# A decode layer on one core: q rows of four groups in four TensorE column groups, h summed in SBUF, a fourth transpose bank, another TensorE order, contiguous FFN stationaries

## The chip, the cores and the metric

The kernel runs on one core of one Trainium2 chip. The metric is the device time of one execution in microseconds (us).

In the views PE is TensorE, PEld its weight loads, ACT is ScalarE and DVE is VectorE, the two engines that here copy TensorE's results out of its PSUM banks into SBUF, the core's memory; SPq is the queue that issues loads and stores. L433 is line 433 of the kernel, x28 a count of instructions. The lines of TensorE (before / after) are: L433 transposes of K, L516 / L518 scores, L538 and L546 / L540 and L573 softmax columns and sums, L561 / L560 products with V, L575 o_columns, L637 / L645 the two FFN input products, L660 / L668 the product with w_down.

## The reference

One decode step of a transformer layer, batch 2, model width 640: layer norm, attention of 32 heads (head width 192) over the last 2,048 cached keys and values, output projection with residual, layer norm, GEGLU feed-forward (FFN) of width 1,536 with residual. Inputs and outputs are bf16.

```
h  = x + attention(layernorm(x), K[:, :, -2048:], V[:, :, -2048:], wq) @ wo
h2 = h + (gelu(layernorm(h) @ w_gate) * (layernorm(h) @ w_up)) @ w_down
```

K and V of the window are 64 tiles each (one per head and batch), 786 KB a tile. With the weights the kernel reads 122.3 MB.

## The kernel before

All loads are issued by one queue (SP) in a fixed order into a ring in SBUF of 110,592 bytes per partition, 18 tiles of K or V. A load may be issued when everything that lies in its place has been used. The order is K of the next group, V of this group, wo of this group, with a block of wq before every fourth K group, and the FFN weights last. A group is four tiles: two heads, two batches (the prediction says "four heads").

```python
GRAN = 768
RING = 18 * 6144
...
        def pump():
            while queue:
                key, off, nbytes, src, shape, i = queue[0]
                old = [q for q in live if q[1] < off + nbytes and off < q[1] + q[2]]
                if any(q[0] not in used for q in old):
                    return
                ...
                toks = [("ring", x) for x in range(off // GRAN, (off + nbytes + GRAN - 1) // GRAN)]
                P.op("sp", lambda e, v=v, src=src: e.dma_start(v, src), W=toks + [("sem", i % NSEM)], ...)
...
            wd = B_w_down.rearrange("(p f) n -> p f n", f=NF)
            for i in range(3):
                load(("wd", i), 2 * 4 * D, wd[:, 4 * i:4 * i + 4, :], ...)
```

The tokens are the kernel's own bookkeeping of who wrote which piece of the ring, in pieces (granules) of 768 bytes. A load waits for the last writer of each of its granules. K, V, wo and wq have sizes that are multiples of 768. The three parts of w_down, 5,120 bytes each, are not, so neighbouring parts share a granule.

TensorE does nearly everything else. K tiles are transposed as f32 pairs into three PSUM banks, which ACT and DVE evict:

```python
        def q_rows(g):                       # [2 x 384]: q of one group, both batches
            for c in range(NC5):
                e.matmul(m1[0:2, 128:512], lhsT=xnT[:, c, :], rhs=wq[:, c, off:off + 384], ...)
            # then ACT copies m1 to qrow
...
        for n in range(4):
            transposes(n)
        for g in range(4):
            q_rows(g)
        q_stationary(0); scores(0); softmax(0); e_columns(0)
        for g in range(NG):                  # 16 groups
            if g + 1 < NG:
                for j in range(4):
                    transposes(4 * (g + 1) + j)
                    if (g + 1) % 4 == 0:
                        q_rows(g + 1 + j)
                q_stationary(g + 1)
            pv(g, 0)
            if g + 1 < NG: scores(g + 1)
            pv(g, 1); pv(g, 2)
            if g + 1 < NG: softmax(g + 1)
            pv(g, 3)                         # and ACT copies the sums to osb
            o_columns(g)
            if g + 1 < NG: e_columns(g + 1)
            oproj(g)                         # accumulates in PSUM bank hps over all groups
        ...
        def ffn_in(bank, key):
            for f in range(NF):
                for c in range(NC5):
                    e.matmul(bank[:, 2 * f:2 * f + 2], lhsT=wv[:, c, f:F:NF], rhs=hnT[:, c, :], ...)
```

## Time and profile before

| | before |
|---|---|
| device time, median of 3 runs | 324.76 us |
| span of the profiled run (its time: 325.54 us) | 323.8 us |
| TensorE busy, mean granted clock | 79%, 0.869 |
| bytes read, mean rate over the span | 122.3 MB, 378 GB/s |

The first view is the page's picture of the kernel before in 40 equal slices (8.1 us each): busy tenths of TensorE, granted TensorE clock in tenths, busy tenths of the DMA engines, and what they moved.

```profile
PE   3665778788887978797887979797987879797784
PEclk9997797979799786979799897979796898979555
DMA  7999999999999999999999999999999999998310
GB/s 274 416 416 414 419 417 416 410 409 419 413 391 329 422 413 419 411 412 414 414 386 413 418 414 417 407 418 414 413 368 419 419 414 415 414 427 371 104 66 0
```

The DMA row says that the engines are busy nearly all the time, and the GB/s row shows small dips. The second view, the waits of TensorE (released by, then us in total, number, longest):

```profile
PE m L575 <- ACT osb L570: 16.1, 16, 1.1
PE tps L433 <- ACT ktr L448: 8.9, 36, 0.3
PE m L546 <- DVE ering L545: 8.4, 16, 0.5
PE m L525 <- DVE mrhs L316: 7.0, 16, 1.1
```

No line of the full waits table before has TensorE waiting for a load. It waits for ACT and DVE, about 16 us, 9 us, 8 us and 7 us. Third, one group in the timeline of TensorE (start, duration, instructions; in brackets the idle time ahead of it and who ended it):

```profile
206.64 0.39 PE L525 MATMUL m<-mrhs,pm 128*128 128x4 f32 x2 [0.41 <-DVE mrhs L316]
206.96 0.52 PE L561 MATMUL ops<-ring,ering 128*32 128x192 bf16 x16
208.53 1.21 PE L575 MATMUL m<-sel,osb 128*128 128x2 f32 x6 [1.06 <-ACT osb L570]
...
210.50 0.38 PE L546 MATMUL m<-zrhs,hm 128*128 128x2 f32 x2 [0.53 <-DVE ering L545]
...
211.34 4.92 PE L433 MATMUL tps<-identf,ring 128*128 128x128 f32 x28
...
217.39 1.53 PE L433 MATMUL tps<-identf,ring 128*128 128x128 f32 x12 [0.26 <-ACT ktr L448]
```

The waits come one after another, and then the transposes run slowly: 28 in 4.92 us at first, then 12 in 1.53 us. The clock record has half the clock (0.50) from 211.85 to 215.27 us. One such group takes 17.03 us. Last, the end of the kernel in the timeline:

```profile
300.40 2.60 PE L561 MATMUL ops<-ring,ering 128*32 128x192 bf16 x64
300.95 5.00 SPq L265 DMA_DIRECT2D ring<-in_B_w_down_dram  x2
309.14 3.72 PE L637 MATMUL sps<-hnT,ring 128*128 128x2 bf16 x60 [0.80 <-DVE hnT L320]
312.71 3.69 PE L637 MATMUL ops<-hnT,ring 128*128 128x2 bf16 x60
316.69 2.56 PE L660 MATMUL m<-uT,ring 128*128 128x2 bf16 x60 [0.28 <-DVE uT L320]
319.49 0.41 SPq L668 DMA_DIRECT2D out_dram<-yT  x1
```

The last products with V (L561) end at 303 us. The completion records of the loads in the trace put the landing of the last V tile at 289.0 us: TensorE is 14 us behind. The parts of w_down land at 300.9, 305.6 and 309.5 us, each issued when the one before has landed.

### The profile page before, as it was taken

What the parts mean: (1) busy time and instruction counts of PE and PEld (TensorE: products, weight loads), DVE (VectorE), ACT (ScalarE), POOL (GpSimd) and SP (SyncE); (2) the same over time, 40 slices, a digit from 0 to 9 for tenths busy, and PEclk for the clock granted to TensorE, in tenths of its full rate; (3) what the DMA queues carried; (4) which work ended last, traced back from release to release, by engine and by line L of the source; (5) the groups of instructions that cost most, each with busy time, mean ns of one, the idle gap of its engine ahead of it and who ended that gap; (6) DMA issues with size and microseconds to landing.
All of it is one profiled execution on the core that took longest, in us unless ns stands there. A gap on an engine that the chain in (4) does not pass through costs nothing.

```text
span 323.8 us, 6976 instructions
## 1 busy us (share of the span) xinstructions
PE 255.5 (79%) x3105; PEld 203.3 (63%) x3105; DVE 126.1 (39%) x340; ACT 112.8 (35%) x150; POOL 3.2 (1%) x9
## 2 busy tenths in 40 slices
PE   3665778788887978797887979797987879797784
PEld 3642758585565858585755758585656757585683
DVE  5621544435343534344342535343333525353120
ACT  2341433324281423333271524243351615242000
POOL 4000000000000000000000000000000000000000
PEclk9997797979799786979799897979796898979555
DMA  7999999999999999999999999999999999998310
GB/s 274 416 416 414 419 417 416 410 409 419 413 391 329 422 413 419 411 412 414 414 386 413 418 414 417 407 418 414 413 368 419 419 414 415 414 427 371 104 66 0
DMA packets 24385, 122.74 MB, mean 379 GB/s; under 512 B 2722, under 2 KB 2724, under 8 KB 24100
## 3 DMA queue, kind: packets, MB, share of 16 engines
q1 hardware_dynamic: 24356, 122.31, 93.3%
q8 instruction: 24, 0.39, 0.5%
q14 instruction: 5, 0.04, 0.0%
HBM read 122.29 MB, written 0.00 MB: 378 GB/s over the span
## 4 chain that ended last, share of the span: by engine, by line
PE 59%; ACT 24%; DVE 12%; issue 3%; POOL 0%; ACTq 0%; POOLq 0%
PE tps L433 27%; ACT ktr L448 16%; PE sps L516 8%; PE m L575 6%; PE m L461 4%; ACT eexp L529 4%; DVE mx L521 3%; PE hps L589 3%; DVE ering L545 2%; PE m L546 2%; PE m L525 2%; ACT osb L570 2%; ACT qrow L466 2%; PE m L538 1%; DVE mrhs L316 1%
## 5 line engine op out<-in xcount | busy, mean ns | idle before, releaser
L433 PE MATMUL tps<-identf,ring 128*128 128x128 f32 x768 | 124.3, 326 | 11.8 <-ACT ktr L448 8.9
L433 PEld LDWEIGHTS tps<-identf,ring 128*128 128x128 f32 x768 | 109.2, 170 | 24.9 <-ACT ktr L448 17.8
L448 ACT ACTIVATE ktr<-tps 128x1024 bf16<-128x1024 bf16 x80 | 80.1, 1022 | 116.2 <-PE tps L433 114.9
L452 DVE COPY ktr<-tps 128x1024 bf16<-128x1024 bf16 x112 | 75.5, 689 | 69.6 <-PE tps L433 68.9
L575 PE MATMUL m<-sel,osb 128*128 128x2 f32 x96 | 19.9, 324 | 16.1 <-ACT osb L570 16.1
L529 ACT ACTIVATE eexp<-sps,nm 128x512 bf16<-128x512 f32 x16 | 11.0, 687 | 59.3 <-DVE nm L527 59.3
L575 PEld LDWEIGHTS m<-sel,osb 128*128 128x128 f32 x96 | 18.6, 270 | 19.9 <-ACT osb L570 19.9
L561 PE MATMUL ops<-ring,ering 128*32 128x192 bf16 x1024 | 30.7, 253 | 0.0
L516 PE MATMUL sps<-ktr,rq 128*32 128x512 bf16 x384 | 26.0, 405 | 5.4 <-ACT ktr L448 4.6
L561 PEld LDWEIGHTS ops<-ring,ering 128*32 128x32 bf16 x1024 | 21.8, 98 | 3.8
L521 DVE TENSOR_REDUCE mx<-sps 128x1 f32<-128x512 f32 x16 | 11.1, 691 | 31.0 <-PE sps L516 31.0
L516 PEld LDWEIGHTS sps<-ktr,rq 128*32 128x32 bf16 x384 | 9.7, 97 | 16.5 <-DVE rq L320 8.6
L461 PE MATMUL m<-ring,xnT 128*2 128x384 bf16 x80 | 17.7, 357 | 2.7 <-ACT qrow L466 2.7
L320 DVE TENSOR_TENSOR rq<-m,mask 128x24 bf16<-128x24 f32 x64 | 7.2, 175 | 18.5 <-PE m L486 18.5
L466 ACT ACTIVATE qrow<-m 2x768 bf16<-2x768 f32 x16 | 12.6, 790 | 4.9 <-PE m L461 4.9
L546 PE MATMUL m<-zrhs,hm 128*128 128x2 f32 x32 | 6.5, 274 | 8.4 <-DVE ering L545 8.4
L320 DVE TENSOR_TENSOR ot<-m,rinv 128x6 bf16<-128x6 f32 x16 | 2.6, 164 | 26.6 <-PE m L575 26.6
L461 PEld LDWEIGHTS m<-ring,xnT 128*2 128x2 bf16 x80 | 5.7, 87 | 11.4 <-ACT qrow L466 4.4
L589 PEld LDWEIGHTS hps<-ot,ring 128*128 128x128 bf16 x240 | 12.1, 134 | 0.3 <-DVE ot L320 0.3
L546 PEld LDWEIGHTS m<-zrhs,hm 128*128 128x128 f32 x32 | 5.2, 203 | 11.4 <-DVE ering L545 11.4
L525 PEld LDWEIGHTS m<-mrhs,pm 128*128 128x128 f32 x32 | 4.8, 188 | 11.3 <-DVE mrhs L316 11.3
L589 PE MATMUL hps<-ot,ring 128*128 128x2 bf16 x240 | 11.6, 177 | 0.3 <-DVE ot L320 0.3
(79 smaller groups left out, 104.6 us busy)
## 6 DMA issues: line engine op xcount, KB each, us to landing
ring<-in_A_k_cache_dram SPq DMA_DIRECT2D x64, 768.0 KB, 14.4
ring<-in_A_v_cache_dram SPq DMA_DIRECT2D x64, 768.0 KB, 15.9
ring<-in_A_wq_dram SPq DMA_DIRECT2D x4, 1920.0 KB, 14.4
ring<-in_A_wo_dram SPq DMA_DIRECT2D x16, 480.0 KB, 14.0
ring<-in_B_w_gate_dram SPq DMA_DIRECT2D x1, 1920.0 KB, 15.3
ring<-in_B_w_up_dram SPq DMA_DIRECT2D x1, 1920.0 KB, 13.4
ring<-in_B_w_down_dram SPq DMA_DIRECT2D x3, 640.0 KB, 4.6
xrow<-in_A_x_dram SPq DMA_DIRECT2D x1, 2.5 KB
```

Source lines behind the costliest of these rows:

```text
L433: ins = e.transpose(tps[bi][:, 128 * u:128 * (u + 1)], kv[:, off:off + 128], identf[:, :])
L448: act(lambda e, c=c, kslot=kslot, bv=bv: e.activation(out=ktr[:, kslot, c, :], in_=bv[:, 0:1024], func=ACT.Copy), W=[("kt", kslot, c)], X= ...
L452: dve(lambda e, c=c, kslot=kslot, bv=bv: e.tensor_copy(ktr[:, kslot, c, :], bv[:, 0:1024]), W=[("kt", kslot, c)], X=[("t", bi)])
L461: ins = e.matmul(m1[0:2, 128:512], lhsT=xnT[:, c, :], rhs=wq[:, c, off:off + 384], start=(c == 0), stop=(c == NC5 - 1))
L466: act(lambda e: e.activation(out=qrow[0:2, g % QS, :, 0:rep, :], in_=m1[0:2, 128:512].rearrange("p (h d) -> p h d", h=2).unsqueeze(2).to_b ...
L516: ins = e.matmul(sps[32 * j:32 * (j + 1), :], lhsT=rq[:, g % 2, j, k, :], rhs=r, start=(k == 0), stop=(k == 5), tile_position=(0, 32 * j))
L521: dve(lambda e: e.tensor_reduce(out=mx[:, :], in_=sps[:, :], axis=AX.X, op=ALU.max), W=["mx"], X=["s"])
L529: act(lambda e: e.activation(out=eexp[:, :], in_=sps[:, :], func=ACT.Exp, bias=nm[:, 0:1], scale=1.0, accum_out=zr[:, 0:1]), R=["nm"], W=[ ...
L546: pe(lambda e: e.matmul(m2[:, 8:10], lhsT=hm[:, :], rhs=zrhs[:, :], start=True, stop=True), R=["hm", "zrhs"], X=["m2"])
L561: ins = e.matmul(ops_[32 * r:32 * (r + 1), 192 * hh:192 * (hh + 1)], lhsT=ering[:, g % 2, col:col + 32], rhs=vv[:, DH * t:DH * (t + 1)], s ...
L575: ins = e.matmul(m1[:, 32 + 2 * kk:34 + 2 * kk], lhsT=osb[:, kk:384:3], rhs=sel[:, :], start=True, stop=True)
L589: ins = e.matmul(hps[:, 2 * c:2 * c + 2], lhsT=wo[:, kk, c:D:NC5], rhs=ot[:, kk, :], start=(g == 0 and kk == 0 and c == 0), stop=(g == NG ...
```

## The change

The intent is to shorten TensorE's work and to take its waits away:

- q rows of four groups are made at once, each group in its own 32-column strip of the array (xnT is padded to 32 columns), with one ACT copy. A wq block is free after one step.
- The softmax columns, o_columns and oproj of the group before are placed between the transposes of the next group, so that DVE and ACT have time to feed them.
- h is summed in SBUF by a small DVE add per group. That frees the PSUM bank hps for a fourth transpose bank.
- The stationaries of the FFN input products are contiguous (columns 128f to 128f+127 instead of every twelfth). To match, w_down is loaded with rows f·128+p: four runs of 1,280 bytes per partition and part instead of one of 5,120.

```diff
-            wd = B_w_down.rearrange("(p f) n -> p f n", f=NF)
+            wd = B_w_down.rearrange("(f p) n -> p f n", p=128)
...
-                    ins = e.matmul(m1[0:2, 128:512], lhsT=xnT[:, c, :], rhs=wq[:, c, off:off + 384],
-                                   start=(c == 0), stop=(c == NC5 - 1))
+                    for r in range(4):
+                        ins = e.matmul(m1[32 * r:32 * (r + 1), 128:512], lhsT=xnT[:, c, :],
+                                       rhs=wq[:, c, 384 * r:384 * (r + 1)], start=(c == 0), stop=(c == NC5 - 1),
+                                       tile_position=(0, 32 * r))
...
-                        ins = e.matmul(hps[:, 2 * c:2 * c + 2], lhsT=wo[:, kk, c:D:NC5], rhs=ot[:, kk, :],
-                                       start=(g == 0 and kk == 0 and c == 0), stop=(g == NG - 1 and kk == 2),
+                        ins = e.matmul(m1[:, 48 + 2 * c:50 + 2 * c], lhsT=wo[:, kk, c:D:NC5], rhs=ot[:, kk, :],
+                                       start=(kk == 0 and c == 0), stop=(kk == 2), skip_group_check=True)
+            dve(tt(hT..., m1[:, 48:58], old..., ALU.add), ...)        # shortened
...
+            if nxt: transposes(4 * g + 4)                             # shortened from here
+            e_columns(g)
+            if nxt: transposes(4 * g + 5)
+            if g > 0: o_columns(g - 1)
+            if nxt and (g + 1) % 4 == 0: q_rows((g + 1) // 4)
+            if nxt: transposes(4 * g + 6)
+            if g > 0: oproj(g - 1)
+            if nxt: transposes(4 * g + 7); q_stationary(g + 1)
+            pv(g, 0); pv(g, 1)
+            if nxt: scores(g + 1)
+            pv(g, 2); pv(g, 3)
+            if nxt: softmax(g + 1)
...
-                        ins = e.matmul(bank[:, 2 * f:2 * f + 2], lhsT=wv[:, c, f:F:NF], rhs=hnT[:, c, :],
+                        ins = e.matmul(bank[:, 2 * f:2 * f + 2], lhsT=wv[:, c, 128 * f:128 * (f + 1)], rhs=hnT[:, c, :],
```

More of the change, by code (lines that the diff above doesn't have):

```diff
@@ L148 @@
 NSEM = 32
-QS = 5
 def bass_sequential_preLN__sliding_block_cached__geglu_ffn__decode_kernel(
@@ L208, in bass_sequential_preLN__sliding_block_cached__geglu_ffn__decode_kernel @@
         lt = sb("lt", [128, 2, B], F32)
-        xnT = sb("xnT", [128, NC5, B], BF16)
+        xnT = sb("xnT", [128, NC5, 32], BF16)
         hnT = sb("hnT", [128, NC5, B], BF16)
         hT = sb("hT", [128, NC5, B], F32)
-        qrow = sb("qrow", [128, QS, 2, rep, DH], BF16)
+        qrow = sb("qrow", [128, 2, 2, rep, DH], BF16)
         rq = sb("rq", [128, 2, 4, 6, 32], BF16)
@@ L217, in bass_sequential_preLN__sliding_block_cached__geglu_ffn__decode_kernel @@
         zr = sb("zr", [128, 1], F32)
-        zrhs = sb("zrhs", [128, 2], F32)
+        zrhs = sb("zrhs", [128, 2, 2], F32)
         rinv = sb("rinv", [128, 2], F32)
@@ L228, in bass_sequential_preLN__sliding_block_cached__geglu_ffn__decode_kernel @@
         uT = sb("uT", [128, NF, B], BF16)
-        tps = [ps(f"tps{i}", [128, 512], F32) for i in range(3)]
+        tps = [ps(f"tps{i}", [128, 512], F32) for i in range(4)]
         sps = ps("sps", [128, 512], F32)
         ops_ = ps("ops", [128, 512], F32)
-        hps = ps("hps", [128, 512], F32)
         m1 = ps("m1", [128, 512], F32)
@@ L352, in bass_sequential_preLN__sliding_block_cached__geglu_ffn__decode_kernel @@
         act(lambda e: e.preload_act_table_set("natural_log_exp_and_others"))
+        dve(lambda e: e.memset(xnT[:, :, :].rearrange("p a b -> p (a b)").bitcast(I32), 0), W=["xnT"])
         def layernorm(src, src_tok, dst, dst_tok):
@@ L369, in layernorm @@
             act(lambda e: e.activation(out=lt[:, 1, :], in_=lt[:, 0, :], func=ACT.Exp, scale=-0.5), R=["lt0"], W=["lt1"])
-            dve(tt(dst[:, :, :], dT[:, 0, :, :], lt[:, 1, :].unsqueeze(1).to_broadcast([128, NC5, B]), ALU.mult),
+            dve(tt(dst[:, :, 0:B], dT[:, 0, :, :], lt[:, 1, :].unsqueeze(1).to_broadcast([128, NC5, B]), ALU.mult),
                 R=["dT0", "lt1"], W=[dst_tok])
@@ L422, in transposes @@
             for c in range(3):
-                bi = tb_count[0] % 3
+                bi = tb_count[0] % 4
                 tb_count[0] += 1
@@ L453, in transposes, with q_rows @@
                         W=[("kt", kslot, c)], X=[("t", bi)])
-        def q_rows(g):
-            wq, wtoks = where["wq", g // 4]
-            off = 384 * (g % 4)
+        def q_rows(J):
+            wq, wtoks = where["wq", J]
             def fn(e):
                 for c in range(NC5):
-                    ins = e.matmul(m1[0:2, 128:512], lhsT=xnT[:, c, :], rhs=wq[:, c, off:off + 384],
-                                   start=(c == 0), stop=(c == NC5 - 1))
+                    for r in range(4):
+                        ins = e.matmul(m1[32 * r:32 * (r + 1), 128:512], lhsT=xnT[:, c, :],
+                                       rhs=wq[:, c, 384 * r:384 * (r + 1)], start=(c == 0), stop=(c == NC5 - 1),
+                                       tile_position=(0, 32 * r))
                 return ins
             pe(fn, R=["xnT"] + wtoks, X=["m1"])
+            done(("wq", J))
             act(lambda e: e.activation(
-                out=qrow[0:2, g % QS, :, 0:rep, :],
-                in_=m1[0:2, 128:512].rearrange("p (h d) -> p h d", h=2).unsqueeze(2).to_broadcast([2, 2, rep, DH]),
-                func=ACT.Copy, scale=SCALE), W=[("qrow", g % QS)], X=["m1"])
-            if g % 4 == 3:
-                done(("wq", g // 4))
+                out=qrow[:, J % 2, :, 0:rep, :],
+                in_=m1[:, 128:512].rearrange("p (h d) -> p h d", h=2).unsqueeze(2).to_broadcast([128, 2, rep, DH]),
+                func=ACT.Copy, scale=SCALE), W=[("qrow", J % 2)], X=["m1"])
         def q_stationary(g):
-            qx = qrow[0:2, g % QS, :, 0:rep, :].rearrange("p h r d -> p h (r d)")
+            p0 = 32 * (g % 4)
+            qx = qrow[p0:p0 + 2, (g // 4) % 2, :, 0:rep, :].rearrange("p h r d -> p h (r d)")
             nk = 6 if words else 3
@@ L485, in fn @@
                             l = qx[:, h, 128 * k:128 * (k + 1)]
-                        ins = e.matmul(m1[:, col:col + 2], lhsT=l, rhs=identb[0:2, 0:2], start=True, stop=True)
+                        ins = e.matmul(m1[:, col:col + 2], lhsT=l, rhs=identb[p0:p0 + 2, p0:p0 + 2], start=True,
+                                       stop=True, tile_position=(p0, 0))
                 return ins
-            pe(fn, R=[("qrow", g % QS), "identb"], X=["m1"])
+            pe(fn, R=[("qrow", (g // 4) % 2), "identb"], X=["m1"])
             for h in range(2):
@@ L530, in softmax @@
                                        accum_out=zr[:, 0:1]), R=["nm"], W=["eexp", "zr"], X=["s"])
-            dve(ts(zrhs[:, :], oh_b[:, :], zr[:, 0:1], ALU.mult), R=["oh_b", "zr"], W=["zrhs"])
+            dve(ts(zrhs[:, g % 2, :], oh_b[:, :], zr[:, 0:1], ALU.mult), R=["oh_b", "zr"], W=[("zrhs", g % 2)])
         def e_columns(g):
@@ L545, in e_columns @@
             dve(lambda e: e.tensor_copy(dst, src), W=[("er", g % 2)], X=["m2"])
-            pe(lambda e: e.matmul(m2[:, 8:10], lhsT=hm[:, :], rhs=zrhs[:, :], start=True, stop=True),
-               R=["hm", "zrhs"], X=["m2"])
-            dve(lambda e: e.reciprocal(rinv[:, :], m2[:, 8:10]), W=["rinv"], X=["m2"])
         def pv(g, j):
@@ L573, in fn @@
             def fn(e):
+                e.matmul(m1[:, 40:42], lhsT=hm[:, :], rhs=zrhs[:, g % 2, :], start=True, stop=True)
                 for kk in range(3):
@@ L577, in fn @@
                 return ins
-            pe(fn, R=["osb", "sel"], X=["m1"])
+            pe(fn, R=["osb", "sel", "hm", ("zrhs", g % 2)], X=["m1"])
+            dve(lambda e: e.reciprocal(rinv[:, :], m1[:, 40:42]), W=["rinv"], X=["m1"])
             dve(tt(ot[:, :, :], m1[:, 32:38].rearrange("p (k b) -> p k b", b=2),
@@ L588, in fn @@
                     for c in range(NC5):
-                        ins = e.matmul(hps[:, 2 * c:2 * c + 2], lhsT=wo[:, kk, c:D:NC5], rhs=ot[:, kk, :],
-                                       start=(g == 0 and kk == 0 and c == 0), stop=(g == NG - 1 and kk == 2),
-                                       skip_group_check=True)
+                        ins = e.matmul(m1[:, 48 + 2 * c:50 + 2 * c], lhsT=wo[:, kk, c:D:NC5], rhs=ot[:, kk, :],
+                                       start=(kk == 0 and c == 0), stop=(kk == 2), skip_group_check=True)
                 return ins
-            pe(fn, R=wtoks + ["ot"], X=["h"])
+            pe(fn, R=wtoks + ["ot"], X=["m1"])
             done(("wo", g))
+            old, tok = (xT, "xT") if g == 0 else (hT, "hT")
+            dve(tt(hT[:, :, :].rearrange("p c b -> p (c b)"), m1[:, 48:58], old[:, :, :].rearrange("p c b -> p (c b)"),
+                   ALU.add), R=[tok], W=["hT"], X=["m1"])
         for n in range(4):
             transposes(n)
-        for g in range(4):
-            q_rows(g)
+        q_rows(0)
         q_stationary(0)
@@ L604, in bass_sequential_preLN__sliding_block_cached__geglu_ffn__decode_kernel @@
         softmax(0)
-        e_columns(0)
         for g in range(NG):
-            if g + 1 < NG:
-                for j in range(4):
-                    transposes(4 * (g + 1) + j)
-                    if (g + 1) % 4 == 0:
-                        q_rows(g + 1 + j)
+            nxt = g + 1 < NG
+            if nxt:
+                transposes(4 * g + 4)
+            e_columns(g)
+            if nxt:
+                transposes(4 * g + 5)
+            if g > 0:
+                o_columns(g - 1)
+            if nxt and (g + 1) % 4 == 0:
+                q_rows((g + 1) // 4)
+            if nxt:
+                transposes(4 * g + 6)
+            if g > 0:
+                oproj(g - 1)
+            if nxt:
+                transposes(4 * g + 7)
                 q_stationary(g + 1)
             pv(g, 0)
-            if g + 1 < NG:
+            pv(g, 1)
+            if nxt:
                 scores(g + 1)
-            pv(g, 1)
             pv(g, 2)
-            if g + 1 < NG:
+            pv(g, 3)
+            if nxt:
                 softmax(g + 1)
-            pv(g, 3)
-            o_columns(g)
-            if g + 1 < NG:
-                e_columns(g + 1)
-            oproj(g)
-        dve(tt(hT[:, :, :].rearrange("p c b -> p (c b)"), hps[:, 0:10], xT[:, :, :].rearrange("p c b -> p (c b)"),
-               ALU.add), R=["xT"], W=["hT"], X=["h"])
+        o_columns(NG - 1)
+        oproj(NG - 1)
         layernorm(hT, "hT", hnT, "hnT")
```

## The prediction

> **What bounds the kernel now.** Two things at nearly the same pace. (1) The load queue: the stretches table shows the 16 DMA engines at a share of 1.0 and about 416 GB/s from 4 us to 296 us, except dips at 96-104, 168-172 and 240-244 us. Completed loads follow each other at 1.885 us per 786 KB tile of K or V (417 GB/s; the Trainium skill, "DMA: Bandwidth & Descriptors", section "Where 436 GB/s comes from", gives 435 as the ceiling, so little is left), 1.19 per wo, 4.89 per wq, 4.6 per FFN input matrix. (2) TensorE: the waits table shows no TensorE wait for data at all. It takes 17.03 us per group of four heads and 20.5 with q_rows, that is 71.6 us per four groups; the loads need 70.0. TensorE lags: the last V tile has landed by about 289 us, its product ends at 303. The chain of waits is TensorE, evictions and softmax (59% PE, 24% ACT, 12% DVE).
>
> At the end, w_down comes in three loads whose ring slots share a bookkeeping granule, so each is issued only when the one before has landed: 300.9, 305.6, 309.5 us.
>
> **What the change does.**
> - q_rows: four rounds of 0.97 us on TensorE plus 0.9 us of waiting for ACT (19.1 to 26.5 us in the timeline) become one of about 1.2 plus 0.8. About 5 us at the start, 2.5 in each of three later groups. wq is freed earlier, so the dip at 96-104 us should go.
> - PE order: takes away, per group, the 1.0 us wait for osb, 0.5 for the zrhs product, most of 0.4 before scores, and part of the 0.5 us eviction stalls (fourth bank). The half-clock stretch after each (0.57-0.7 at the start of each transpose phase; "TensorE: Matmul & The Clock Gate", Part 1, says idle windows gate the clock, and this trace agrees) should shrink. Estimate: 13-15 us of TensorE work per group, about 25 us less in all.
> - h in SBUF: one more 0.17 us DVE add per group, hidden.
> - Contiguous FFN stationaries: 60 matmuls from 3.7 toward 2.6 us each time, but off the path afterwards. w_down now comes as 512 runs of 1,280 B instead of 128 of 5,120 per load. 3,072 B packets take 125 ns and 6,144 B ones 236, so about 60 ns each: +0.35 us per load, perhaps +0.5.
>
> **On the critical path.** The 25 us are not earned: the kernel becomes bound by its loads. Nominal load times in order put w_down's first landing at 293.9 us; instruction fetches delay the stream by about 3.5 (6.9 us of excess are seen before, of which 3.5 near 100 us are ring stalls that go); the smaller runs add 0.4: about 298. Then two serial loads (4.7 and 3.9 before) at about 5.1 and 4.4: 307.6. The last 20 matmuls 1.1, yT and the output 4.5: span 313.2. Measured times lie about 1 us above the span: **314.0 us**, 80% range 311.0 to 318.5. Chances: faster by over 2% 0.88, within 2% 0.10, slower 0.02.
>
> **What would show it.** TensorE waits for loads of K, V and w_down; the ring waits of the queue (97 us for transposes now) collapse; DMA share 1.0 up to 296 us without the dip near 100; w_gate's product starts near 293 us instead of 309; the FFN input products get shorter without moving the end; the chain of waits ends with the third w_down load.
>
> **What would make it wrong.** Evictions on ACT (1.02 us for five of twelve banks) or a half clock during data waits keep TensorE above 17.5 us per group (then 318-322). Small runs cost more than estimated in the serial w_down loads (316-318). Instruction fetches disturb less (311).

## The result, and the profile after

The changed kernel takes 313.88 us (median of 4 runs, 313.73 to 314.2); before took 324.81 (4 runs, 324.13 to 325.04). The ratio is 0.9668, 95% interval 0.9651 to 0.9685. A ratio is the mean time of one kernel's fast runs over that of the other's fast runs of the same rounds, so it is not quite the ratio of the medians. The span of the profiled run is 312.0 us, the mean clock 0.848.

The page's picture of the changed kernel (slices of 7.8 us):

```profile
PE   3769795826988595955989597945959795976632
PEclk9999899975999787796999778895977889795555
DMA  7999999999999999999999999999999999999732
GB/s 272 415 416 413 417 416 417 414 405 417 417 415 416 413 417 415 418 403 417 417 415 415 417 414 415 418 406 417 414 417 417 414 415 413 417 414 431 320 116 82
```

The dips in GB/s are gone (no slice in the middle under 403), and TensorE now has slices with five tenths of work or less. The waits of TensorE have changed kind:

```profile
PE tps L433 <- DMA ring<-in_A_k_cache_dram: 42.0, 15, 7.1
PE ops L560 <- DMA ring<-in_A_v_cache_dram: 13.1, 13, 1.4
PE m L668 <- DMA ring<-in_B_w_down_dram: 7.2, 2, 4.1
PE m L527 <- DVE mrhs L314: 3.7, 8, 1.1
```

Three kinds of load account for 62 us of TensorE's waiting; there were none before. The last V tile lands at 286.6 us, and its product comes right behind it. The end of the kernel in the timeline:

```profile
286.62 0.83 PE L560 MATMUL ops<-ring,ering 128*32 128x192 bf16 x16 [1.06 <-DMA ring<-in_A_v_cache_dram]
294.29 1.76 PE L645 MATMUL sps<-hnT,ring 128*128 128x2 bf16 x60 [0.80 <-DVE hnT L318]
297.02 1.76 PE L645 MATMUL ops<-hnT,ring 128*128 128x2 bf16 x60 [0.97 <-DMA ring<-in_B_w_up_dram]
298.62 4.62 SPq L263 DMA_DIRECT2D ring<-in_B_w_down_dram  x2
302.92 0.93 PE L668 MATMUL m<-uT,ring 128*128 128x2 bf16 x20 [4.15 <-DMA ring<-in_B_w_down_dram]
306.91 1.76 PE L668 MATMUL m<-uT,ring 128*128 128x2 bf16 x40 [3.05 <-DMA ring<-in_B_w_down_dram]
308.91 0.39 SPq L676 DMA_DIRECT2D out_dram<-yT  x1
```

And the last pieces of the chain of waits, in order of time (start, us, what; 144 pieces, of which the last DMA pieces and the last matmuls are shown):

```profile
273.33 25.27 DMA ring<-in_B_w_down_dram
...
298.62 4.17 DMA ring<-in_B_w_down_dram
...
302.87 3.99 DMA ring<-in_B_w_down_dram
...
306.91 1.77 PE m L668 x40
```

The chain ends in three w_down loads in a row. The first lands in the full stream. The other two are each issued after the one before has landed and take 4.2 and 4.0 us, for 655 KB that the full stream delivers in about 1.6 us. A detail that the prediction had not seen: the product of the first part starts at 302.92, when the *second* part has landed, and the last 40 matmuls start together. The shared granule makes readers wait for the neighbour's load as well.

### The profile page after: what moved, and what is told of

Its sections match the earlier page's. It is cut to its first block, busy times and chain, and to the rows that moved or that the text cites. A ratio compares the mean times of both kernels' runs of the same rounds, so it can differ in the third digit from the quotient of the medians.

```text
span 312.0 us, 7012 instructions
## 1 busy us (share of the span) xinstructions
PE 225.7 (72%) x3105; PEld 195.1 (63%) x3105; DVE 125.8 (40%) x356; ACT 105.9 (34%) x138; POOL 3.2 (1%) x9
## 4 chain that ended last, share of the span: by engine, by line
DMA 72%; PE 20%; SPq 6%; issue 1%; DVE 0%
DMA ring<-in_A_k_cache_dram 50%; PE tps L433 12%; DMA ring<-in_A_v_cache_dram 12%; DMA ring<-in_B_w_down_dram 11%; SPq L263 6%; PE m L575 2%; PE ops L560 1%; PE sps L518 1%; PE m L590 1%; PE m L540 1%; PE m L668 1%; PE m L487 0%; PE m L461 0%; PE m L573 0%; SPq L320 0%
## 5 line engine op out<-in xcount | busy, mean ns | idle before, releaser
L433 PE MATMUL tps<-identf,ring 128*128 128x128 f32 x768 | 121.1, 320 | 44.4 <-DMA ring<-in_A_k_cache_dram 42.0
L569 ACT ACTIVATE osb<-ops 128x384 f32<-128x384 f32 x16 | 7.8, 490 | 57.2 <-PE ops L560 57.2
L580 DVE RECIPROCAL rinv<-m 128x2 f32<-128x2 f32 x16 | 2.7, 170 | 31.2 <-PE m L575 31.2
L590 PEld LDWEIGHTS m<-ot,ring 128*128 128x128 bf16 x240 | 11.8, 129 | 1.1 <-DVE ot L318 1.1
L590 PE MATMUL m<-ot,ring 128*128 128x2 bf16 x240 | 11.7, 177 | 0.9 <-DVE ot L318 0.9
L547 DVE COPY ering<-m 128x64 bf16<-128x64 bf16 x16 | 7.0, 436 | 6.5 <-PE m L540 6.5
L540 PE MATMUL m<-identb,eexp 128*128 128x128 bf16 x64 | 8.8, 281 | 1.2 <-ACT eexp L531 1.2
L314 DVE TENSOR_SCALAR zrhs<-oh_b,zr 128x2 f32<-128x2 f32 x16 | 3.6, 228 | 13.5 <-ACT eexp L531 13.5
L527 PE MATMUL m<-mrhs,pm 128*128 128x4 f32 x32 | 6.2, 263 | 3.7 <-DVE mrhs L314 3.7
L529 DVE TENSOR_REDUCE nm<-m 128x1 f32<-128x4 f32 x16 | 2.6, 161 | 15.0 <-PE m L527 15.0
## 6 DMA issues: line engine op xcount, KB each, us to landing
ring<-in_A_k_cache_dram SPq DMA_DIRECT2D x64, 768.0 KB, 20.6
```

Of the source, the lines that this page charges most:

```text
L433: ins = e.transpose(tps[bi][:, 128 * u:128 * (u + 1)], kv[:, off:off + 128], identf[:, :])
L527: pe(lambda e: e.matmul(m2[:, 0:4], lhsT=pm[:, :], rhs=mrhs[:, :], start=True, stop=True), R=["pm", "mrhs"], X=["m2"])
L540: ins = e.transpose(ev[:, 128 * cc:128 * (cc + 1)], eexp[:, 128 * cc:128 * (cc + 1)], identb[:, :])
L590: ins = e.matmul(m1[:, 48 + 2 * c:50 + 2 * c], lhsT=wo[:, kk, c:D:NC5], rhs=ot[:, kk, :], start=(kk == 0 and c == 0), stop=(kk == 2), skip ...
```

## The experiments

Theory: before, TensorE sets the pace; after, the load stream does, and the end is set by the serial w_down loads. Several parts of the change can then each reach the floor, and their gains don't add. Rivals: the load queue bound both kernels; or each part earns its own share; or the contiguous FFN stationaries gave what was earned at the end. Landing times below are from the completion records of the loads in each trace.

### Controls: the changed kernel again, and the loads taken away from both kernels

Control, no edit:

> The changed kernel itself, as a control on the same chip as the three runs beside it. All theories: 313.9 us, within 0.5.

Measured: 313.92 us (313.68 to 314.19), ratio 0.9666. As expected.

For the next two, half of each K and V tile is loaded and read twice. The arithmetic is wrong; TensorE's instructions are the same in number and shape.

```diff
-   load(("k", n), 2 * T * DH, kv_src(A_k_cache, n), lambda v: v)          # and the same for v
+   load(("k", n), T * DH, kv_src(A_k_cache, n)[:, 0:T * DH // 2], lambda v: v)
-   off = 384 * u + 128 * c
+   off = 384 * (u % 2) + 128 * c
-   rhs=vv[:, DH * t:DH * (t + 1)]
+   rhs=vv[:, DH * (t % 8):DH * (t % 8 + 1)]
```

On the kernel before:

> Kernel before, wrong on purpose: only the first half of every K and V tile is loaded, and read twice; TensorE does the same work. Theory (before, TensorE is the slower of the two all the way): 322 to 325 us although 41% of the bytes are gone. Rival (the load queue bound the kernel before): about 200 to 220 us.

Measured: 325.8 us (323.22 to 326.31), ratio 1.0023, interval 0.9981 to 1.0064; 0.8 above the expected range. With 72.4 MB instead of 122.7 the time is the same. So TensorE and its waits set the pace before, and the busy queue was not the bound.

On the changed kernel:

> Changed kernel with the same halved loads, wrong on purpose. Theory (the changed kernel is bound by its loads, with TensorE at 12.5 to 13 us per group of its own): about 250 us (240 to 262), TensorE bound, so the new order is worth some 70 us of TensorE time of which 11 were earned. Rival (the change made TensorE only some 11 to 25 us faster, as the prediction's estimate had it): 300 to 314 us.

Measured: 230.13 us (229.65 to 230.34), ratio 0.7078. The theory holds, but TensorE was faster than its number: a miss of 20 us. The waits table shows no TensorE wait for a load in this run either. One group in its timeline, to set beside the group of before:

```profile
82.66 0.39 PE L527 MATMUL m<-mrhs,pm 128*128 128x4 f32 x2 [0.39 <-DVE mrhs L314]
82.90 1.51 PE L433 MATMUL tps<-identf,ring 128*128 128x128 f32 x12
...
84.47 1.75 PE L433 MATMUL tps<-identf,ring 128*128 128x128 f32 x12
...
94.56 0.39 PE L527 MATMUL m<-mrhs,pm 128*128 128x4 f32 x2 [0.39 <-DVE mrhs L314]
```

From 82.66 to 94.56 is 11.90 us for a group that took 17.03. One wait of 0.39 us is left, and every tile's 12 transposes take 1.5 to 1.75 us. The stretch from 60 to 180 us of the two kernels with halved loads (before first, changed second; after the length come busy us and count of PE, PEld, DVE, ACT and POOL, and the last three numbers are granted clock, DMA share, GB/s):

```profile
60.00:180.00 120.00, 99.65 (x1237) 77.81 (x1234) 47.41 (x121) 44.64 (x61) 0.00 (x0) 0.89 0.68 226
```

```profile
60.00:180.00 120.00, 114.29 (x1806) 97.17 (x1805) 66.69 (x186) 63.05 (x80) 0.00 (x0) 1.00 0.96 367
```

Without gaps the clock is granted in full, 1.00 instead of 0.89. The Trainium skill, "TensorE: Matmul & The Clock Gate", Part 1, describes a gate that watches how busy the array is; the trace agrees as far as the two numbers go. So the waits cost twice: by themselves, and by the slow stretch that follows. How the gate decides isn't shown here (see the last section).

### The parts alone, on the kernel before

The contiguous FFN layout alone (the w_down rearrangement and the stationaries of the last lines of the diff above):

> Kernel before with only the contiguous FFN layout. Theory: there TensorE comes last (w_down has landed at 309.5 us, its product starts at 316.7), so the two input products' 3.9 us are earned in full: about 320.9 us. Rival (small w_down runs cost what the products gain, or the layout is off the path here too): 323.5 to 325.

Measured: 319.86 us (318.35 to 320.5), ratio 0.9847 (interval 0.9816 to 0.9878, so clear of noise, though under 2%), 4.9 us faster than before. TensorE comes last there, so its 3.9 us count in full. The other microsecond is the output store; see below.

The q rows of four groups alone (with xnT, qrow and q_stationary as in the change; old order, three banks, hps, old FFN):

> Kernel before with only q rows of four groups at once. Theory (a floor set by the loads, so parts do not add): TensorE starts its groups some 6 to 11 us earlier and takes 70 us per four groups, which is the pace of the loads, so most of the whole gain comes from this part alone: about 315.5 us (314 to 318). Rival (parts add, each earns its share of TensorE time, and q rows are about half of the 25 us): 319.5 us.

Measured: 314.96 us (314.87 to 316.04), ratio 0.9711. The third w_down part lands at 307.7 us, 0.8 us after that of the changed kernel, in a profiled run that was the slowest of the five (316.04; the others took 314.87 to 315.0). The waits for ACT and DVE are still there (15.6 us for osb, 8.4 for the softmax columns); it just starts earlier and no longer falls behind.

The new order, the fourth bank and h in SBUF alone (old q rows, four in a row at the start and one after each transposed tile of every fourth group; old FFN):

> Kernel before with only the new TensorE order, the fourth transpose bank and h in SBUF; old q rows, old FFN layout. Theory: TensorE falls below the pace of the loads in every group and catches up with them from its late start, so this part alone too reaches the floor of the changed kernel: about 314.2 us (313.5 to 316). Rival (parts add): about 319 us.

Measured: 315.22 us (314.4 to 316.15), ratio 0.9711; third w_down part at 307.1 us.

Subtracting each from the before median of its batch, 324.71, the three parts earn 4.9, 9.8 and 9.5 us alone, 24 in sum. Together they earn 10.9. Either of the last two is enough to reach the floor: the changed kernel with the old FFN layout, which both of them have, takes 314.85 us (below).

The fourth bank undone in the changed kernel:

```diff
-        tps = [ps(f"tps{i}", [128, 512], F32) for i in range(4)]
+        tps = [ps(f"tps{i}", [128, 512], F32) for i in range(3)]
-                bi = tb_count[0] % 4
+                bi = tb_count[0] % 3
```

> Changed kernel with three transpose banks instead of four. Theory (bound by the loads, TensorE has 62 us of waits for data to give): within 0.5 us of the changed kernel, 313.4 to 314.4; stalls on evictions come back in the waits, up to 0.5 us per group, and the waits for K loads shrink by as much. Rival (the bank is part of what made the kernel faster): 316 us or more.

Measured: 314.02 us (313.91 to 314.21), ratio 0.9668. The bank earns nothing here. TensorE waits for K loads 42.9 us instead of 42.0. The eviction waits came back only in part (the transposes' waits for DVE are 3.4 us instead of 1.9), less than the expectation allowed; with the new order, and TensorE waiting for loads anyway, three banks nearly suffice. What the bank is worth to TensorE alone was not run, nor were the order and h in SBUF taken apart.

### The floor: the serial w_down loads

```diff
-GRAN = 768
+GRAN = 256
```

All sizes in the ring are multiples of 256, so no two loads share a granule, and nothing else changes.

> Changed kernel with a finer bookkeeping granule, so that the three w_down loads no longer wait for one another. Theory (the end is set by the serial w_down loads): the loads land about 1.6 us apart, the third near 302 us instead of 306.9, time about 308.8 us, 5.1 below the changed kernel. Rival (the end is set by TensorE's own chain from the last V tile, and the w_down wait only looks like the cause): within 1 us of 313.9.

Measured: 308.13 us (307.98 to 308.3), ratio 0.9488. Its end in the timeline:

```profile
299.00 0.96 PE L668 MATMUL m<-uT,ring 128*128 128x2 bf16 x20 [0.28 <-DVE uT L318]
300.26 0.96 PE L668 MATMUL m<-uT,ring 128*128 128x2 bf16 x20 [0.30 <-DMA ring<-in_B_w_down_dram]
301.92 0.96 PE L668 MATMUL m<-uT,ring 128*128 128x2 bf16 x20 [0.70 <-DMA ring<-in_B_w_down_dram]
303.13 0.39 SPq L676 DMA_DIRECT2D out_dram<-yT  x1
```

The parts land at 298.6, 300.2 and 301.9 us, and each product follows its own part. The third landing is 5.0 us earlier than in the changed kernel, and only 20 matmuls (0.96 us), not 40 (1.76), come after it: 5.8 us in all, 0.7 more than expected. The false dependency is the cause of the floor at the end, and this version beats both kernels.

The old FFN layout in the changed kernel, then in the one with the finer granule (the first and the last pair of lines of the diff, reversed):

> Changed kernel with the old FFN layout (strided stationaries, w_down in 5,120-byte runs). Theory: the two input products take 3.7 us each again instead of 1.76, but end before the third w_down load lands, so the time stays within 0.5 us of the changed kernel, 313.4 to 314.4. Rival (the contiguous stationaries shorten the end by the 3.9 us that the products lose): 317.8 us.

Measured: 314.85 us (314.44 to 314.93), ratio 0.9695, 0.9 above the control. The rival's 3.9 us are refuted: uT is ready at 301.5 us and the third part lands at 306.3. But 0.9 is more than the 0.5 that the theory allowed.

> The finer granule with the old FFN layout. Theory: with the w_down loads no longer last, the FFN products are on the path: uT is ready at about 302 us, then 60 matmuls of 2.6 us, so about 1.7 us slower than the finer granule alone, near 310.5 us. Rival (the layout of the FFN never matters): the same as the finer granule alone.

Measured: 310.83 us (310.78 to 310.86), ratio 0.9571: 2.7 us slower than the finer granule alone, where 1.7 was expected. Direction right, again a microsecond too much.

The extra microsecond is in the output store, 2.5 KB at the very end. These are the lines of the list of loads and stores (size, us from issue to landing) of before, of the changed kernel and of the run that follows:

```profile
out_dram<-yT SPq DMA_DIRECT2D x1, 2.5 KB, 3.9
```

```profile
out_dram<-yT SPq DMA_DIRECT2D x1, 2.5 KB, 2.7
```

```profile
out_dram<-yT SPq DMA_DIRECT2D x1, 2.5 KB, 3.8
```

To separate the two halves of the layout, only w_down's rows are loaded as before in the changed kernel; the result is wrong (relative error 1.39).

```diff
-            wd = B_w_down.rearrange("(f p) n -> p f n", p=128)
+            wd = B_w_down.rearrange("(p f) n -> p f n", f=NF)
```

> Changed kernel with only the rows of w_down loaded as before (5,120-byte runs), stationaries contiguous; wrong on purpose, since the rows no longer match. It separates the two halves of the old FFN layout, which cost 0.9 us where 0.5 at most was expected: in the traces the output store lands after 3.9 to 4.2 us in all six kernels with the old layout and after 2.6 to 3.0 in all six with the new. Theory W (the store's time goes with the way w_down is loaded): store near 4.0 us, time about 314.8. Theory S (it goes with the strided stationaries): store near 2.7 us, w_down about 0.4 us earlier, time about 313.5.

Measured: 314.54 us (314.29 to 315.08), ratio 0.9687; store 3.8 us, with w_down's third part 0.4 us earlier. Theory W: the store goes with the way w_down is loaded, not with the stationaries. Why a load that ended before should change a later store is not settled. The two forms differ in the number of runs (1,152 more in the new form) and in where rows lie; no run separates these.

### What still delays the stream

Added up from the load times of undisturbed stretches (1.885 us a tile, 1.19 a wo, 4.89 a wq, 4.6 an FFN input matrix, 1.53 for the first w_down part), that first part would land at 293.9 us before and, counted from a first landing 0.1 us later, at 294.1 after. It lands at 300.9 before and 298.6 after, 7.0 and 4.5 us late. Around 100 us, where the ring stalled before, the dips are gone; as stretches of the kernel before and of the changed kernel (last two numbers: DMA share, GB/s):

```profile
96.00:100.00 4.00, 3.01 (x78) 1.75 (x80) 0.69 (x5) 1.11 (x2) 0.00 (x0) 1.00 0.77 273
```

```profile
96.00:100.00 4.00, 3.29 (x75) 2.38 (x77) 1.71 (x6) 1.29 (x2) 0.00 (x0) 1.00 1.01 413
```

What stays are four delays of 0.6 to 1.6 us, at 24, 27, 123 and 223 us. Instruction fetches of 16 KB, 24 in all, stand in the DMA records, each holding one engine for about 1.07 us; three of them, at 22.96, 119.66 and 221.23 us, come just before these delays. The Trainium skill, "Runtime: NRT & Kernel Launch", section "Instruction fetch mechanics", says that instructions come in blocks of 16 KiB, 256 instructions each, over DMA, and that the cost is mostly hidden. The block size agrees; that it is hidden is in doubt here, where every engine is busy all the time.

The kept traces say more about these delays. Each load leaves sixteen completion records, and it has landed with the last of them. In the changed kernel the sixteen lie within 0.5 us of each other up to 21.5 us; for w_gate they spread from 286.9 to 292.4. Against the same sum of load times the first of these is 0.6 us early and the last 4.4 us late: the stream as a whole is not slowed, a part of the sixteen falls behind, and a load waits for the last. The last one slips at the same fetches in every run: in all ten traces of kernels at their load floor it slips by 0.7 to 1.7 us at the 9th and again at the 17th fetch, and in the run below, which has more fetches, at the 9th, 17th and 25th, which come at 95.9, 167.6 and 243.3 us instead. The delay at 24 us is most likely something else: in the kernel before, a like one of 0.8 us at 26 us comes ahead of the first fetch (30.3 us).

As a test, the 12 small matmuls of q_stationary are issued six times instead of once, which changes no value:

```diff
             def fn(e):
-                for h in range(2):
+                for _rep in range(6):
+                  for h in range(2):
                     ...
```

> Changed kernel with the 12 small matmuls of q_stationary done six times instead of once: 60 more matmuls and weight loads per group, 2.2 us of TensorE time per group (36 us in all) and about 7 more instruction fetches of 16 KB. Theory A (TensorE has slack, and instruction fetches delay the load stream in proportion): about 315.2 us, 1.3 above the changed kernel, first w_down landing near 300.1 instead of 298.7. Theory B (slack, but fetches are not what delays the stream): 313.9. Rival (TensorE still sets the pace): 330 or more.

Measured: 316.64 us (315.37 to 316.86), ratio 0.9729, 2.8 above the changed kernel's 313.88. The changed kernel was not run beside it; by the ratios to before (0.9729 and 0.9668) the difference is 2.0 us. There are 32 fetches instead of 24. The first w_down part lands at 300.0, as theory A said. The rest is in the third part, which takes 5.5 us instead of 4.1 with a fetch recorded at 307.4 us, in the middle of it. The two groups of run times, two near 315.5 and four near 316.7, would fit such a hit or miss, but only one run was profiled. The slow profiled run with q rows alone shows the same: a fetch at 299.7 us, and the part in flight took 5.1 us. This also shows TensorE's slack: 60 matmuls more per group, and its waits for K loads shrink from 42.0 to 27.6 us. Since the fetches came with more TensorE work, fetches as the cause are supported rather than isolated; that the slips moved with the fetches is the stronger evidence. Why a slip exceeds the 1.07 us of a fetch is open.

## Why the prediction was right, point by point

The time was 313.88 us against 314.0 predicted, well inside the range, and the mechanism held: the kernel became bound by its loads, with the serial w_down loads last. The terms of the sum:

| step | predicted | measured |
|---|---|---|
| first w_down part lands | 298 us | 298.6 us |
| second, third part | +5.1, +4.4 | +4.2, +4.1 |
| last matmuls, yT and output | 5.6 | 5.1 |
| span to device time | 1.0 | 1.8 in the profiled run |

The errors are within a microsecond each and cancel. That the time was hit to 0.1 us is luck. (The 1.0 in the last row came from the median time of before, 324.76, beside the span of a slower run, 325.54.)

- "What bounds the kernel now. Two things at nearly the same pace": too weak. With 41% of the bytes gone the time did not move; TensorE alone was the bound, and the loads came next, close behind.
- "about 25 us less in all" is the term that was badly mis-sized. With the loads halved in both, TensorE's own time went from 325.8 to 230.1 us, 96 us. The prediction costed the waits (about 2.5 us per group) but only an unsure share of the slow-clock stretch: "13-15 us of TensorE work per group" was 11.9. Its total doesn't follow from its own terms either: 13 to 15 instead of 17.03 is 32 to 64 us over 16 groups. At the start, "about 5 us" for the q rows was 5.5 (from 19.14 to 26.59 us before, from 17.53 to 19.48 after), but the group loop began 10.8 us earlier, at 23.3 instead of 34.1: an earlier start, shorter scores (1.56 us instead of 2.75) and softmax columns that moved into the loop were not in the sum. The error did not reach the time, because all beyond the first 11 us was idle time at the floor.
- "The 25 us are not earned: the kernel becomes bound by its loads": right; shown by the waits, by the halved loads, and by the parts that don't add.
- "the ring waits of the queue (97 us for transposes now) collapse": wrong. The queue's waits for transposes went from 97.2 to 78.4 us. A queue that fills the ring waits for free places also when the loads are the bound; the time of a K load from issue to landing only grew, from 14.4 to 20.6 us (medians).
- "wq is freed earlier, so the dip at 96-104 us should go": the dip went, but the earlier release isn't needed. With the new order and the old q rows, 96 to 100 us has 416 GB/s too.
- "w_down ... issued only when the one before has landed": right and decisive. Freeing the loads earned 5.8 us. That readers share the wait was missed.
- "from 3.7 toward 2.6 us each time, but off the path afterwards": the products went to 1.76 us. Off the path, right: what the layout earned in the changed kernel is the store's time, which the prediction didn't have.
- "+0.35 us per load, perhaps +0.5" for the small runs: the packets took 61 ns on average, as estimated, yet the load took only 0.1 us longer in the full stream (1.66 against 1.53, both with the finer granule). With the finer granule a packet took 57 ns on average; 32 of them for each of 16 engines would be 1.8 us, more than the 1.66 of the load, so packet times overlap in part.
- "instruction fetches delay the stream by about 3.5": the excess after was 4.5 us, 0.1 of it from w_down's runs; that fetches cause most of it is supported by one run and by where the slips come in ten traces.

## What to carry to other kernels

A DMA queue at full share isn't by itself a bound: look whether anybody waits for a load, and if in doubt halve the bytes. When two limits are close, cost a change only down to the second one; parts that each reach it don't add, and work beyond it (here 85 us of TensorE time) earns nothing until the second limit moves. A load has landed with the last of its sixteen completions: compare the first with the last before calling the whole stream slow. At the new limit, look at what the last loads wait for: a coarse dependency granule cost 5.8 us here, more than half of what the whole change earned.

## What the Trainium skill lacked or had wrong

- "DMA: Bandwidth & Descriptors", "Where 436 GB/s comes from", says that for HBM to SBUF the HBM side (about 358 GB/s) binds. Here one core read at 417 GB/s in the full stream (786 KB each 1.885 us), nearer to the 435 that the same section gives for the port side. The page has the condition elsewhere: the section "Measured (HBM→SBUF, 128 partitions, SWDGE, issued from GpSimd)" gives 425 GB/s for one core and says that about 358 is left when both cores of the domain stream. The sentence in question lacks it.
- "TensorE: Matmul & The Clock Gate", Part 4, says that the full clock doesn't engage for transposes. Here the granted clock was 1.00 from 60 to 180 us in the changed kernel with halved loads, where transposes are about half of TensorE's time; and in the kernel before it came back to full at 215.27 us, after 3.4 us in which TensorE did transposes alone.
- The same page, Part 1, puts the half rate after an idle window of about 3.4 us. Here it came without one: in the 3.41 us ahead of 211.85 us TensorE was busy for 2.80, and no wait in a group was longer than 1.1 us.
- The same page, "Weight-path perf modes", admits strided stationaries and gives no cost for the step there. Here 60 pairs of weight load and small matmul took 1.76 us with contiguous columns, 2.56 with a step of 5 and 3.7 with a step of 12, at a granted clock of 0.5.
- "Runtime: NRT & Kernel Launch", "Instruction fetch mechanics", calls the cost of a fetch mostly hidden. It lacks the case of a saturated load queue: 24 fetches of 1.07 us on one engine each stood beside loads whose last completion was 4.5 us late, in steps at the 1st, 9th and 17th fetch, and with 32 fetches the first w_down part landed another 1.4 us later.
- No page that was read has that a 2.5 KB store can take 2.7 or 3.9 us depending on how an earlier load was laid out; the cause stays open.
